# One table of places set anew for a fused attention, Fourier-mix and feed-forward kernel

## The chip, the core and the metric

The kernel runs on one core of one Trainium2 chip. The core has five engines with in-order queues: PE (TensorE, matrix products), DVE (VectorE), ACT (ScalarE), POOL (GpSimd) and SP (SyncE, which here only issues transfers). They meet at semaphores; transfers run on 16 DMA engines that all queues share. The metric is the device time of one execution in microseconds (us), lower is better. All times below are from the profiled execution or from the timed runs.

## What is computed

For a batch of 8 sequences of 576 tokens, 8 heads of 64:

```
q_d, k_d, v_d = mean over groups of 4 tokens      # 144 tokens
out_up    = repeat(softmax_attention(q_d, k_d, v_d), 4)
out_local = softmax_attention(q, k, v) where |i - j| < 4
x   = heads side by side of (out_up + out_local)  # 8 x 576 x 512
u   = x + real(fft over channels(fft over tokens(x)))
un  = (u - mean) / sqrt(var + 1e-6)
out = u + relu(un @ w1) @ w2                      # 512 -> 2048 -> 512
```

## The kernel before, in words

The work is cut into steps, each a method that issues a few instructions on one engine. Every step is put on a list by `at`, and the list is sorted and issued; so every engine gets its instructions in the order of that list, and works through them in that order. A step stands at the number that the table `TURNS` gives it (a *place*); a step that has none stands at a planned time `t`, and all steps with a place come before all without.

- **Unit** (40 of them, 5 for each batch): the local attention of 128 tokens. `load` brings q and k (`qkT`, 6 buffers), `load_v` brings v (`vaug`, 6 buffers), `sum_in` adds up groups of 4 tokens into `sums` on DVE (L603), `scores` puts a mask and the products into two banks of PSUM (L613, L620), `maxima` (DVE, L632), `exps` (ACT, L639), `transpose_p` (PE, L652), `copy_p` (ACT), `values` (PE, L680), `result` (DVE, L697 to L700; into the tiles `xa` and `xb`).
- **Pooled** (8, one for each batch): the attention over the pooled tokens, in three groups g. `scores` (L473) needs the sums of all five units of its batch; `pool_v` (L447) needs the `vaug` of all five. The group 2's `result` leaves the tile `rest` (L540), and `pack` (L564 and L553) then issues eight small transfers of it on SP. `store` issues the other pooled rows.
- **Mix** (8): the two Fourier transforms as matrix products (L793, L808, L832) with folding before and unfolding after on DVE and POOL.
- **Quarter** (64): one quarter of a feed-forward weight tile is fetched and cut into a high and a low float32r part.
- **Block** (9): the feed-forward part of 512 tokens. For each of 16 slices f of the hidden width, `first` (L1172), `high`, `low`, `second` (L1192 to L1194). Blocks 3 to 8 make the first product by seven smaller products (`open`, `more`, `close`, L1110) whose results `save` (ACT, L1130) and `combine` (DVE, L1135) join; their weights are prepared once by **Differences** (8 groups, L952 to L975), written to DRAM, and streamed back for each block.

SP issues all of the loads named and most stores, in the order of the list. An issue whose input or buffer is not ready holds back every issue behind it.

Before, the table goes up to place 1573, the first five slices of blocks 0 and 1 and eleven more of block 0 with their loads, and a few more; block 1's rest, block 2, Differences and everything after it stand at planned times.

```
place = next(places.get(name, iter(())), None)
events.append((place is None, t if place is None else place, len(events), partial(fn, *args)))
...
for *_, fn in sorted(events, key=lambda e: e[:3]):
    fn()
```

Of the kernel before, what the change touches and what calls it, by code (L numbers as in the profile page):

```python
# [26 lines left out]
    "Pooled.pool_v": (49, 130, 261, 398, 518, 677, 799, 920),  # L27
    "Pooled.copy_v": (50, 132, 263, 399, 520, 680, 800, 925),
    "Pooled.scores": (
        33, 17, 16, 163, 77, 105, 276, 200, 221, 419, 328, 348, 548, 483, 498, 675, 614, 633, 818, 744, 758,  # L30
        950, 862, 882,
    ),
    "Pooled.maxima": (
        43, 19, 20, 166, 83, 109, 283, 207, 224, 427, 332, 353, 552, 488, 511, 697, 617, 641, 823, 746, 770,
        952, 865, 891,
    ),
    "Pooled.exps": (
        46, 23, 30, 173, 86, 115, 288, 216, 231, 435, 339, 361, 558, 502, 519, 703, 620, 650, 837, 756, 780,
        954, 869, 896,
    ),  # L40
# [8 lines left out]
    "Pooled.values": (
        88, 51, 62, 198, 133, 142, 320, 264, 277, 445, 400, 413, 602, 522, 537, 727, 684, 698, 852, 803, 821,  # L50
        965, 927, 949,
    ),
    "Pooled.result": (
        93, 54, 71, 202, 155, 154, 323, 273, 284, 454, 408, 416, 605, 542, 544, 730, 694, 701, 856, 809, 826,
        972, 935, 951,
    ),
    "Pooled.store": (97, 212, 392, 463, 626, 750, 878, 975),
    "Pooled.pack": (100, 213, 342, 493, 624, 747, 871, 977),
    "Mix.half_sum": (
        120, 91, 125, 247, 252, 253, 352, 355, 372, 513, 515, 526, 636, 658, 662, 763, 762, 786, 887, 905, 904,  # L60
        1000, 1004, 1003,
    ),
    "Mix.half_difference": (
        112, 95, 111, 219, 255, 280, 356, 379, 380, 504, 529, 531, 646, 663, 665, 767, 795, 794, 885, 918, 915,
        999, 994, 1009,
    ),
    "Mix.channels": (
# [4 lines left out]
    ),  # L72
    "Mix.fold": (
# [4 lines left out]
    ),  # L78
    "Mix.split_z": (84, 137, 191, 287, 362, 382, 535, 534, 681, 686, 777, 836, 930, 921, 983, 1014),
    "Mix.sequence_z": (165, 311, 440, 573, 705, 841, 960, 1016),  # L80
    "Mix.z_high": (175, 316, 457, 587, 715, 847, 1022, 1054),
    "Mix.z_low": (182, 326, 474, 590, 720, 859, 1031, 1064),
    "Mix.sequence": (
        181, 180, 178, 179, 330, 331, 329, 327, 480, 481, 465, 466, 608, 615, 576, 586, 740, 743, 741, 739, 860,
        861, 879, 881, 1010, 1011, 987, 1007, 1071, 1070, 1107, 1102,
    ),
    "Mix.sequence_out": (193, 189, 341, 337, 484, 470, 621, 597, 755, 754, 868, 886, 1021, 1024, 1120, 1111),
    "Mix.mix": (
        239, 266, 227, 260, 350, 368, 385, 387, 366, 418, 497, 521, 500, 536, 642, 654, 631, 685, 676, 678, 772,
        804, 768, 773, 895, 900, 928, 957, 893, 901, 1069, 1072, 1068, 1029, 1131, 1157, 1186, 1214, 1185, 1213,  # L90
    ),
    "Mix.even_out": (
        262, 235, 363, 389, 390, 501, 508, 648, 634, 679, 778, 775, 898, 933, 922, 1079, 1080, 1143, 1208, 1194,
    ),
    "Mix.unfold": (
        281, 286, 270, 271, 375, 374, 404, 403, 425, 426, 539, 543, 549, 551, 660, 659, 702, 695, 689, 690, 814,
        813, 788, 787, 911, 910, 969, 968, 934, 939, 1098, 1134, 1101, 1099, 1178, 1180, 1233, 1232, 1217, 1219,
    ),
    "Mix.store_mixed": (307, 423, 625, 708, 876, 976, 1159, 1235),
    "Mix.store_local": (143, 150, 244, 309, 394, 462, 564, 572, 707, 668, 752, 783, 877, 973, 998, 1006),  # L100
    "Mix.store_ends": (496, 835, 974, 1220),
    "Unit.load": (
        2, 3, 1, 0, 7, 40, 41, 58, 57, 38, 99, 146, 147, 145, 148, 243, 149, 246, 208, 245, 396, 424, 421, 391,
        461, 568, 567, 569, 571, 595, 623, 669, 667, 709, 670, 785, 748, 832, 784, 833,
    ),
    "Unit.sum_in": (
        9, 10, 11, 12, 13, 42, 53, 64, 66, 73, 168, 172, 183, 184, 185, 282, 297, 300, 321, 324, 432, 449, 450,
        475, 477, 579, 583, 591, 593, 607, 688, 696, 733, 734, 735, 829, 830, 853, 855, 857,
    ),
    "Unit.load_v": (  # L110
        8, 36, 37, 39, 4, 5, 102, 98, 101, 103, 211, 242, 144, 209, 241, 308, 345, 393, 395, 346, 397, 490, 492,
        491, 494, 565, 627, 628, 596, 666, 751, 671, 753, 749, 782, 834, 874, 875, 872, 873,
    ),
    "Unit.scores": (
        14, 15, 25, 61, 48, 74, 104, 117, 119, 141, 199, 220, 236, 237, 319, 291, 365, 384, 420, 447, 468, 517,
        545, 585, 601, 610, 629, 652, 699, 725, 726, 781, 802, 820, 825, 864, 899, 943, 940, 956,
    ),
# [24 lines left out]
    "constants": (79,),
    "clear_yz": (136,),
    "close_b": (988,),
    "close_a": (1013,),
    "close_e": (1132,),
    "close_d": (1256,),
    "Block.load": (
        570, 798, 912, 566, 765, 884, 563, 796, 917, 344, 612, 916, 1042, 1077, 1087, 1034, 1060, 1085, 1043,
        1095, 1135, 1040, 1117, 1148, 1553, 1561, 1566, 1555, 1562, 1570, 1556, 1563, 1572, 1557, 1565, 1573,  # L150
    ),
    "Block.stats": (970, 909, 996, 971, 1137, 1162, 1164, 1179, 1571),
    "Block.norm": (991, 1005, 1028, 1048, 1150, 1175, 1177, 1216),
    "Block.turn": (1008, 1015, 1030, 1073, 1155, 1183, 1215, 1237),
    "Block.turn_high": (1020, 1038, 1057, 1081, 1171, 1191, 1225, 1240),
    "Block.turn_low": (1032, 1052, 1066, 1097, 1181, 1200, 1231, 1246),
    "Block.first": (
        1108, 1109, 1126, 1130, 1184, 1267, 1266, 1294, 1293, 1318, 1319, 1257, 1322, 1405, 1432, 1374, 1448,
        1484, 1483, 1512, 1529, 1538, 1539, 1554, 1564,
    ),  # L160
    "Block.high": (
        1112, 1115, 1153, 1168, 1209, 1273, 1269, 1303, 1307, 1351, 1361, 1381, 1391, 1415, 1440, 1417, 1460,
        1490, 1491, 1517, 1532, 1548, 1549, 1558, 1567,
    ),
    "Block.low": (
        1125, 1128, 1165, 1176, 1218, 1281, 1279, 1312, 1317, 1356, 1369, 1394, 1399, 1425, 1445, 1447, 1467,
        1497, 1499, 1526, 1534, 1550, 1551, 1559, 1568,
    ),
# [1284 lines left out]
```

## Time and profile before

| | |
|---|---|
| Timed runs | 1124.72 us median of 3 (1123.99 to 1129.9) |
| Profiled execution, span | 1124.3 us; the profile states no other time of it |
| PE busy | 1070.8 us, 95% of the span |
| DVE busy | 637.6 us, 57%; but 44 of every 50 us between 150 and 300 us |
| Attention and mix | about 0 to 320 us |
| Blocks 0 to 2 | about 300 to 590 us, blocks 3 to 8 from 590 us on |

A busy share is of the whole span or of a named window. A wait is told with the engine that waited, the operation that came next there and what released it. The granted clock of TensorE is given as a share of full speed: 1.00 is 2.4 GHz and 0.50 is 1.2 GHz.

### The profile page before, as it was taken

The numbers are of one execution on the slowest core, as the hardware profiler recorded it, in microseconds if no ns is written. First come the engines' busy times: TensorE is split into PE (matmuls) and PEld (weight loads), VectorE is DVE, ScalarE is ACT, GpSimd is POOL, SyncE is SP. The second block draws the span as 40 slices with busy tenths as digits, with TensorE's granted clock in tenths as the row PEclk, the third lists the DMA queues.
The fourth block names the chain that finished last, engine by engine and source line by source line (L and its number), as shares of the span: only waits on it lengthen the run. The fifth ranks groups of instructions, "written<-read, shape, count | busy, mean of one in ns | idle before, by whom it ended". The sixth has DMA issues, their size and how long they took to land.

```text
span 1124.3 us, 24306 instructions
## 1 busy us (share of the span) xinstructions
PE 1070.8 (95%) x9316; PEld 899.0 (80%) x9316; DVE 637.6 (57%) x1298; ACT 401.0 (36%) x1122; POOL 352.0 (31%) x501
## 2 busy tenths in 40 slices
PE   7787998999999999999999999999999999999998
PEld 5565766777778888887788889888989889889997
DVE  4778889988999885452314533443443343353333
ACT  4756565675444442132221231232232132132121
POOL 1313231233475553487331140331231331222000
PEclk9999999999999999999999999999999999999999
DMA  6545647676685444478709845955955975875641
GB/s 246 187 168 189 223 140 226 226 229 175 181 193 169 123 122 140 111 241 279 194 1 278 245 152 166 314 171 160 298 194 162 259 236 159 221 252 183 216 160 38
DMA packets 121451, 214.36 MB, mean 191 GB/s; under 512 B 14576, under 2 KB 30992, under 8 KB 121208
## 3 DMA queue, kind: packets, MB, share of 16 engines
q1 hardware_dynamic: 110056, 191.97, 52.0%
q0 software_dynamic: 11280, 20.84, 10.2%
q8 instruction: 74, 1.21, 0.4%
q14 instruction: 41, 0.34, 0.1%
HBM read 166.86 MB, written 45.42 MB: 189 GB/s over the span
## 4 chain that ended last, share of the span: by engine, by line
PE 67%; DMA 13%; DVE 9%; SPq 4%; POOL 3%; issue 3%; ACT 2%; DVEq 0%; ACTq 0%; POOLq 0%
PE banks L1110 18%; PE banks L1192 10%; PE banks L1193 10%; PE banks L1194 10%; PE banks L1172 7%; PE banks L793 3%; DMA w1l<-ut 2%; DMA qkT<-in_qk_dram 2%; DMA w1h<-ut 2%; PE banks L832 2%; PE banks L522 1%; DMA raw<-in_wq_dram 1%; DMA vaug<-in_vw_dram 1%; PE banks L1039 1%; DMA out_dram<-ut 1%
## 5 line engine op out<-in xcount | busy, mean ns | idle before, releaser
L1192 PE MATMUL banks<-w2h,hh 128*128 128x512 f32 x576 | 228.4, 397 | 0.7 <-ACT hh L1176 0.7
L1194 PE MATMUL banks<-w2h,hl 128*128 128x512 f32 x576 | 225.0, 391 | 0.8 <-DVE hl L1180 0.8
L1193 PE MATMUL banks<-w2l,hh 128*128 128x512 f32 x576 | 225.4, 391 | 0.0
L1176 ACT ACTIVATE hh<-row 128x512 fp32r<-128x512 f32 x96 | 60.6, 632 | 285.8 <-DVE row L1135 194.2
L1135 DVE TENSOR_TENSOR row<-wt,banks 128x256 f32<-128x256 f32 x192 | 80.4, 419 | 142.9 <-PE banks L1110 138.7
L1180 DVE SCALAR_TENSOR_TENSOR hl<-row,hh 128x512 fp32r<-128x512 f32 x96 | 68.9, 718 | 118.8 <-ACT hh L1176 118.8
L1194 PEld LDWEIGHTS banks<-w2h,hl 128*128 128x128 f32 x576 | 108.2, 188 | 25.5 <-DVE hl L1180 1.7
L1192 PEld LDWEIGHTS banks<-w2h,hh 128*128 128x128 f32 x576 | 108.5, 188 | 20.7 <-ACT hh L1176 1.1
L1193 PEld LDWEIGHTS banks<-w2l,hh 128*128 128x128 f32 x576 | 108.6, 188 | 19.2
L1172 PE MATMUL banks<-unT,w1h 128*128 128x512 f32 x384 | 102.3, 392 | 0.6 <-DVE unT L1048 0.6
L1172 PEld LDWEIGHTS banks<-unT,w1h 128*128 128x128 f32 x384 | 71.7, 188 | 16.4 <-DVE unT L1048 1.0
L1009 POOL DMA_DIRECT2D ut<-ux x40 | 35.7, 1034 | 152.4 <-DMA ut<-um 124.7
L1180 DVE SCALAR_TENSOR_TENSOR hl<-banks,hh 128x512 fp32r<-128x512 f32 x48 | 32.8, 688 | 77.5 <-ACT hh L1176 77.5
L639 ACT ACTIVATE sb<-banks,mx 128x64 f32<-128x64 f32 x320 | 70.0, 330 | 1.3
L1130 ACT COPY wt<-banks 128x256 f32<-128x256 f32 x96 | 35.8, 372 | 95.4 <-PE banks L1110 95.4
L793 PE MATMUL banks<-seq,f 128*128 128x290 f32 x256 | 67.0, 412 | 2.1 <-ACT sb L639 1.4
L1110 PE MATMUL banks<-w1h,w1h 128*128 128x256 f32 x384 | 62.0, 283 | 3.1 <-DMA w1h<-ut 3.0
L1110 PE MATMUL banks<-w1h,w1l 128*128 128x256 f32 x384 | 62.6, 285 | 2.4 <-DMA w1l<-ut 2.0
L1110 PE MATMUL banks<-unT,w1h 128*128 128x256 f32 x432 | 63.4, 283 | 0.0
L1110 PE MATMUL banks<-unT,w1l 128*128 128x256 f32 x432 | 63.2, 282 | 0.0
L1110 PEld LDWEIGHTS banks<-unT,w1h 128*128 128x128 f32 x432 | 59.8, 190 | 3.9
L1110 PEld LDWEIGHTS banks<-unT,w1l 128*128 128x128 f32 x432 | 59.8, 191 | 3.7
(122 smaller groups left out, 1929.1 us busy)
## 6 DMA issues: line engine op xcount, KB each, us to landing
w1l<-ut SPq DMA_DIRECT2D x96, 256.0 KB
w1h<-ut SPq DMA_DIRECT2D x96, 256.0 KB
qkT<-in_qk_dram SPq DMA_DIRECT2D x40, 512.0 KB
w1h<-ub SPq DMA_DIRECT2D x72, 256.0 KB
w1l<-ub SPq DMA_DIRECT2D x72, 256.0 KB
raw<-in_wq_dram SPq DMA_DIRECT2D x64, 256.0 KB
vaug<-in_vw_dram SPq DMA_DIRECT2D x40, 260.0 KB
out_dram<-ut SPq DMA_DIRECT2D x36, 256.0 KB
```

Of the source, the lines that this page charges most:

```text
L639: nc.scalar.activation(out=self.sb[:, hp, z], in_=self.sc[:, z, hp], func=AF.Exp, scale=0.125, bias=self.mx[:, z, hp : hp + 1],)
L793: nc.tensor.matmul(y, l, r, start=(i == 0), stop=(i == len(mms) - 1))
L1009: nc.gpsimd.dma_start(out=to, in_=ux[b][k0 : k0 + m, :], accum_op=ALU.add)
L1110: nc.tensor.matmul(into, w[:, y, c, :], both[z][:, c, :], start=(start and i == 0), stop=(i == len(mms) - 1), skip_group_check=True)
L1130: nc.scalar.copy(out=joins[k].bitcast(F32), in_=self.ps[x])
L1135: nc.vector.tensor_add(out=place(to), in0=place(a), in1=self.ps[x])
L1172: nc.tensor.matmul(hps, a[:, c, :], unT[:, x, c, :], start=(i == 0), stop=(i == len(mms) - 1))
L1176: nc.scalar.activation(out=hh, in_=self.hps[f], func=AF.Relu)
L1180: nc.vector.scalar_tensor_tensor(out=hl, in0=self.hps[f], scalar=0.0, in1=self.hh[f].bitcast(F32), op0=ALU.max, op1=ALU.subtract)
L1192: nc.tensor.matmul(acc, hh, w2h, start=start, stop=False)
L1193: nc.tensor.matmul(acc, hh, w2l, start=False, stop=False)
L1194: nc.tensor.matmul(acc, hl, w2h, start=False, stop=stop)
```

## The change

All 1574 places are replaced by 1898 new ones. New in the table are the rest of block 1, block 2, Differences, the loads and preparation of block 3, and the first six weight streams of block 3. No operation is added, taken away or altered: each engine issues the same instructions, in as great a number, in another order. Two entries, as an example:

```
     "Unit.load_v": (
-        8, 36, 37, 39, 4, 5, 102, 98, 101, 103, 211, 242, 144, 209, 241, 308, 345, 393, 395, 346, 397, 490, 492,
...
+        18, 45, 20, 49, 37, 81, 83, 105, 24, 100, 196, 162, 122, 194, 199, 363, 344, 302, 310, 312, 461, 470,
+        480, 443, 347, 555, 491, 663, 648, 625, 742, 776, 754, 746, 783, 883, 902, 855, 830, 695,
...
     "Block.second": (
-        1140, 1156, 1182, 1212, 1236, 1295, 1296, 1320, 1321, 1363, 1375, 1404, 1406, 1433, 1449, 1482, 1485,
-        1513, 1514, 1530, 1537, 1552, 1560, 1569,
...
+        1752, 1769, 1775, 1789, 1801, 1807, 1825, 1835, 1856, 1864, 1873, 1877, 1881, 1884,
```

In the changed file the table is 94 lines longer, so a line L591 of before is L685 there.

Three places show how the order moves. The first is DVE's queue from its first real work on, before the change; `sums` are the five `sum_in` of batch 0, `mx` a unit's maxima and `mxd` the pooled maxima:

```order
L603 TENSOR_REDUCE sums<-qkT 128x8x32 x2
L603 TENSOR_REDUCE sums<-qkT 128x8x15
L603 TENSOR_REDUCE sums<-qkT 128x8x17
L603 TENSOR_REDUCE sums<-qkT 128x8x32 x2
L632 TENSOR_REDUCE mx<-banks 128x8
L478 TENSOR_REDUCE mxd<-banks 128x4 x2
L632 TENSOR_REDUCE mx<-banks 128x8
```

The same place of DVE's queue after the change:

```order
L697 TENSOR_REDUCE sums<-qkT 128x8x32
L726 TENSOR_REDUCE mx<-banks 128x8
L697 TENSOR_REDUCE sums<-qkT 128x8x32 x2
L726 TENSOR_REDUCE mx<-banks 128x8
L697 TENSOR_REDUCE sums<-qkT 128x8x32
L697 TENSOR_REDUCE sums<-qkT 128x8x15
L697 TENSOR_REDUCE sums<-qkT 128x8x17
L726 TENSOR_REDUCE mx<-banks 128x8
L572 TENSOR_REDUCE mxd<-banks 128x4
```

The maxima of three units have moved in between the sums, and unit 0's block of q and k, which was issued third, is now issued first.

The second place is SP's queue around the `pack` of batch 0 (`xa<-rest` and `ud_57<-rest`, four pairs), before the change; the `vaug` behind it are those of units 8, 6 and 9:

```order
L591 DMA vaug<-in_vw_dram 128x520
L587 DMA qkT<-in_qk_dram 128x1024
L564 DMA xa<-rest 32x128
L553 DMA ud_57<-rest 29x128
...
L591 DMA vaug<-in_vw_dram 128x520 x3
L884 DMA ux_65<-xa 56x3x512
```

The same place of SP's queue after the change; the `vaug` ahead are those of units 5 and 6, the two behind those of units 9 and 7:

```order
L685 DMA vaug<-in_vw_dram 128x520 x2
L681 DMA qkT<-in_qk_dram 128x1024
L658 DMA xa<-rest 32x128
L647 DMA ud_57<-rest 29x128
...
L685 DMA vaug<-in_vw_dram 128x520 x2
L647 DMA ud_57<-odt 30x512
```

Two loads of batch 1 stand behind the `pack` in place of three, and the `rest` that the `pack` waits for is made earlier: in the new order seven steps of DVE that stood ahead of it stand behind it (the `result` of units 2 and 3, the `maxima` of unit 5 and of the pooled group 0 of batch 1, one `half_sum` and two `channels`). On PE two steps that stood ahead of `pool_v` of batch 1 stand behind it (`scores` of unit 8, `transpose_p` of unit 6).

The third place is SP's queue around the `pack` of batch 1, before the change; the `vaug` behind it are two of the five of batch 2:

```order
L564 DMA xa<-rest 32x128
L553 DMA ud_58<-rest 29x128
L331 DMA raw<-in_wq_dram 128x512
L591 DMA vaug<-in_vw_dram 128x520 x2
L587 DMA qkT<-in_qk_dram 128x1024
```

The same place of SP's queue after the change:

```order
L685 DMA vaug<-in_vw_dram 128x520
L425 DMA raw<-in_wq_dram 128x512
L685 DMA vaug<-in_vw_dram 128x520 x2
L681 DMA qkT<-in_qk_dram 128x1024 x2
L658 DMA xa<-rest 32x128
L647 DMA ud_58<-rest 29x128
```

All v of batch 2 is now asked for ahead of the `pack` of batch 1.

## Rows read from the trace of the kernel before

**Rows 1.** The page: busy time, share and instructions of each engine.

```profile
PE 1070.8 (95%) x9316; PEld 899.0 (80%) x9316; DVE 637.6 (57%) x1298; ACT 401.0 (36%) x1122; POOL 352.0 (31%) x501
```

**Rows 2.** Windows: length, PE, PEld, DVE, ACT, POOL busy (count), clock, DMA share, GB/s.

```profile
0.00:50.00 50.00, 36.54 (x773) 28.24 (x773) 28.75 (x55) 27.95 (x102) 9.31 (x24) 1.00 0.60 209
50.00:100.00 50.00, 40.63 (x699) 28.98 (x699) 39.46 (x79) 27.35 (x95) 13.73 (x18) 0.93 0.57 191
100.00:150.00 50.00, 45.02 (x768) 33.73 (x769) 42.47 (x93) 28.61 (x103) 11.85 (x19) 0.97 0.60 197
150.00:200.00 50.00, 45.77 (x826) 33.98 (x828) 45.08 (x90) 32.62 (x119) 15.56 (x22) 1.00 0.63 194
200.00:250.00 50.00, 47.54 (x915) 35.32 (x906) 44.07 (x92) 33.24 (x122) 13.78 (x18) 1.00 0.77 236
250.00:300.00 50.00, 47.37 (x816) 35.55 (x815) 44.41 (x101) 25.30 (x89) 18.54 (x25) 1.00 0.59 159
300.00:320.00 20.00, 19.41 (x87) 15.17 (x86) 18.40 (x35) 8.86 (x23) 15.46 (x23) 1.00 0.88 214
320.00:590.00 270.00, 267.32 (x1194) 218.58 (x1193) 154.35 (x295) 87.86 (x206) 146.55 (x213) 1.00 0.54 156
590.00:1124.00 534.00, 521.18 (x3263) 469.47 (x3261) 220.62 (x464) 129.22 (x272) 107.27 (x144) 1.00 0.66 203
```

**Rows 3.** Waits of PE, 0 to 320 us: total us, times, longest.

```profile
PE banks L447 <- DMA vaug<-in_vw_dram: 5.9, 3, 3.0
PE banks L473 <- DVE sums L603: 3.8, 2, 3.6
```

**Rows 4.** Timeline of DVE, 7 to 20 and 40 to 46 us: start, us, instruction, idle before.

```profile
8.28 1.22 DVE L603 TENSOR_REDUCE sums<-qkT 128x256 f32<-128x1024 f32 x1 [7.33 <-DMA qkT<-in_qk_dram]
9.83 4.66 DVE L603 TENSOR_REDUCE sums<-qkT 128x256 f32<-128x1024 f32 x5 [0.33 <-DMA qkT<-in_qk_dram]
...
43.53 0.29 DVE L540 TENSOR_TENSOR rest<-banks,rsd 128x128 f32<-128x128 f32 x1
```

**Rows 5.** Timeline of PE, 7 to 24, 44 to 60 and 98 to 108 us.

```profile
7.69 0.43 PE L613 MATMUL banks<-maskb,identb 64*64 64x256 bf16 x4 [2.23 <-DMA maskb<-in_c_mask_dram]
...
14.54 2.41 PE L473 MATMUL banks<-sums 64*64 64x160 f32 x32 [3.56 <-DVE sums L603]
...
45.91 0.66 PE L652 MATMUL banks<-ident,sb 128*128 128x128 f32 x4 [0.44 <-DVE xb L700]
...
48.47 0.73 PE L447 MATMUL banks<-vaug,poolm 128*32 128x260 f32 x4
52.24 3.02 PE L447 MATMUL banks<-vaug,poolm 128*32 128x260 f32 x16 [3.04 <-DMA vaug<-in_vw_dram]
...
101.41 0.69 PE L680 MATMUL banks<-vaug,pT 64*64 64x65 f32 x32 [1.68 <-DVE odt L540]
```

**Rows 6.** Windows of PE alone: length, busy us (count), clock, DMA share, GB/s.

```profile
50.00:52.50 2.50, 0.26 (x4) 0.73 0.88 296
52.50:55.00 2.50, 2.50 (x16) 0.50 0.87 270
```

**Rows 7.** Timeline of SP's issues, 24 to 90 us: start, us, line, transfer.

```profile
43.88 0.62 SPq L564 DMA_DIRECT2D xa<-rest  x1
...
48.23 1.82 SPq L591 DMA_DIRECT2D vaug<-in_vw_dram  x3
...
87.56 0.90 SPq L591 DMA_DIRECT2D vaug<-in_vw_dram  x2
```

**Rows 8.** Chain that ended last, 76 to 95 us: start, us, what.

```profile
77.88 6.06 DMA vaug<-in_vw_dram
```

**Rows 9.** Waits of PE, 86 to 96 us.

```profile
PE banks L447 <- DMA vaug<-in_vw_dram: 2.2, 1, 2.2
```

**Rows 10.** Groups of DVE by form, 0 to 50 us: busy, mean ns, idle before.

```profile
L632 DVE TENSOR_REDUCE mx<-banks 128x8 f32<-128x512 f32 x7 | 4.8, 683 | 0.7 <-PE banks L620 0.7
...
L700 DVE TENSOR_TENSOR xb<-banks,rs 128x512 f32<-128x512 f32 x2 | 1.4, 692 | 0.1
```

More of the change, by code (lines that the diff above doesn't have):

```diff
@@ L26 @@
 TURNS = {
-    "Pooled.pool_v": (49, 130, 261, 398, 518, 677, 799, 920),
-    "Pooled.copy_v": (50, 132, 263, 399, 520, 680, 800, 925),
+    "Pooled.pool_v": (
+        55, 125, 253, 392, 518, 667, 797, 918,
+    ),
+    "Pooled.copy_v": (
+        59, 129, 262, 399, 521, 670, 806, 926,
+    ),
     "Pooled.scores": (
-        33, 17, 16, 163, 77, 105, 276, 200, 221, 419, 328, 348, 548, 483, 498, 675, 614, 633, 818, 744, 758,
-        950, 862, 882,
+        41, 22, 34, 150, 78, 115, 263, 204, 230, 411, 346, 361, 523, 483, 501, 671, 627, 646, 803, 755, 764,
+        934, 866, 899,
@@ L48 @@
+        953, 886, 941,
     ),
     "Pooled.values": (
[L50 to L51 removed]
+        72, 62, 66, 211, 145, 151, 316, 275, 285, 446, 403, 432, 576, 527, 551, 720, 675, 717, 856, 809, 845,
+        967, 927, 947,
     ),
     "Pooled.result": (
[L54 to L56 removed]
@@ L57 @@
-    "Pooled.store": (97, 212, 392, 463, 626, 750, 878, 975),
-    "Pooled.pack": (100, 213, 342, 493, 624, 747, 871, 977),
+        79, 63, 71, 217, 147, 161, 322, 277, 297, 456, 405, 448, 580, 536, 556, 721, 679, 719, 869, 811, 857,
+        970, 935, 956,
+    ),
+    "Pooled.store": (
+        109, 187, 404, 453, 653, 768, 868, 973,
+    ),
+    "Pooled.pack": (
+        95, 229, 332, 489, 606, 734, 891, 976,
+    ),
     "Mix.half_sum": (
-        120, 91, 125, 247, 252, 253, 352, 355, 372, 513, 515, 526, 636, 658, 662, 763, 762, 786, 887, 905, 904,
-        1000, 1004, 1003,
+        108, 134, 127, 258, 237, 254, 360, 395, 373, 515, 506, 517, 642, 639, 643, 751, 788, 774, 907, 913,
+        932, 993, 980, 996,
@@ L81 @@
-    "Mix.z_high": (175, 316, 457, 587, 715, 847, 1022, 1054),
-    "Mix.z_low": (182, 326, 474, 590, 720, 859, 1031, 1064),
[4 rows of a table added]
+    ),
+    "Mix.split_z": (
+        133, 157, 189, 267, 380, 421, 468, 558, 637, 700, 787, 815, 922, 939, 1002, 1006,
+    ),
+    "Mix.sequence_z": (
+        185, 290, 458, 559, 714, 824, 986, 1015,
+    ),
+    "Mix.z_high": (
+        207, 304, 469, 573, 715, 835, 991, 1053,
+    ),
+    "Mix.z_low": (
+        214, 311, 486, 578, 725, 843, 1013, 1083,
+    ),
     "Mix.sequence": (
-        181, 180, 178, 179, 330, 331, 329, 327, 480, 481, 465, 466, 608, 615, 576, 586, 740, 743, 741, 739, 860,
-        861, 879, 881, 1010, 1011, 987, 1007, 1071, 1070, 1107, 1102,
-    ),
@@ L148 @@
+        609, 621, 628, 640, 741, 710, 730, 773, 761, 841, 864, 876, 889, 894, 946, 961, 984, 975, 992,
+    ),
+    "constants": (
+        135,
+    ),
+    "clear_yz": (
+        176,
+    ),
+    "close_b": (
+        1008,
+    ),
+    "close_a": (
+        1014,
+    ),
+    "close_e": (
+        1119,
+    ),
+    "close_d": (
+        1317,
+    ),
     "Block.load": (
-        570, 798, 912, 566, 765, 884, 563, 796, 917, 344, 612, 916, 1042, 1077, 1087, 1034, 1060, 1085, 1043,
-        1095, 1135, 1040, 1117, 1148, 1553, 1561, 1566, 1555, 1562, 1570, 1556, 1563, 1572, 1557, 1565, 1573,
-    ),
@@ L152 @@
[L152 to L156, printed above, removed]
[3 rows of a table added]
+    ),
+    "Block.stats": (
+        995, 877, 909, 890, 1131, 1163, 1192, 1158, 1655, 1620, 1649, 1610, 1806, 1823, 1814, 1837,
+    ),
+    "Block.norm": (
+        1016, 1025, 1065, 1050, 1149, 1169, 1205, 1168, 1666, 1628, 1659, 1617, 1808, 1827, 1820, 1839,
+    ),
@@ L171 @@
-        1513, 1514, 1530, 1537, 1552, 1560, 1569,
-    ),
-    "Block.finish": (1259, 1280, 1282, 1313, 1368, 1446, 1373, 1370, 1540, 1541, 1542, 1543),
-    "Block.store": (1544, 1545, 1546, 1547),
[3 rows of a table added]
+    ),
+    "Block.finish": (
+        1242, 1289, 1287, 1249, 1356, 1357, 1535, 1371, 1566, 1569, 1571, 1570, 1738, 1702, 1723, 1708, 1885,
+        1888, 1892, 1895,
+    ),
+    "Block.store": (
+        1612, 1599, 1575, 1574, 1750, 1714, 1724, 1757, 1889, 1891, 1894, 1896,
+    ),
+    "Block.turn_copy": (
+        1838, 1846, 1836, 1844,
+    ),
@@ new lines @@
+    "Block.add_up": (
+        1841, 1848,
+    ),
+    "Block.sum_high": (
+        1868, 1859, 1849, 1857, 1853, 1858, 1852, 1861,
+    ),
+    "Block.sum_low": (
+        1893, 1890, 1876, 1869, 1887, 1897, 1875, 1886,
+    ),
+    "Differences.rejoin": (
+        1549, 1559, 1609, 1657, 1690, 1729, 1753, 1793,
+    ),
+    "Differences.differ": (
+        1550, 1593, 1647, 1675, 1703, 1731, 1762, 1803,
+    ),
+    "Differences.high": (
+        1576, 1551, 1553, 1562, 1623, 1595, 1598, 1597, 1648, 1651, 1663, 1658, 1695, 1683, 1687, 1679, 1706,
+        1710, 1704, 1717, 1735, 1733, 1740, 1739, 1767, 1781, 1771, 1764, 1810, 1804, 1809, 1816,
+    ),
@@ L175 @@
+    "Differences.low": (
+        1585, 1554, 1565, 1579, 1630, 1641, 1613, 1608, 1650, 1653, 1665, 1660, 1700, 1694, 1696, 1685, 1707,
+        1713, 1719, 1721, 1742, 1749, 1743, 1744, 1776, 1797, 1780, 1786, 1813, 1817, 1812, 1828,
+    ),
+    "Differences.keep": (
[4 rows of a table added]
+    ),
+    "Block.stream": (
+        1770, 1783, 1787, 1860, 1819, 1821,
+    ),
     "Quarter.fetch": (
[4 rows of a table removed]
[4 rows of a table added]
     ),
     "Quarter.size": (
[4 rows of a table removed]
[4 rows of a table added]
     ),
     "Quarter.clamp": (
[4 rows of a table removed]
[4 rows of a table added]
     ),
     "Quarter.join": (
[4 rows of a table removed]
[4 rows of a table added]
     ),
     "Quarter.high": (
[4 rows of a table removed]
[4 rows of a table added]
```

109 lines of the change are left out of this document (57 added, 52 removed), and 82 rows, old and new, of the table TURNS.

## The prediction

> **What bounds the kernel now.** I began with the busy shares [rows 1]: PE is busy for 1070.8 of 1124.3 us, so at most 53.5 us are to be had without faster operations, and an order can't make an operation faster. The windows [rows 2] say where they lie. Of the 270 us from 320 to 590 us PE idles for 2.7 (267.32 busy), and after that, where the table reaches only the first weights, for 12.8. So the change is decided in the first 320 us: PE idles there for 13.5, 9.4, 5.0, 4.2, 2.5 and 2.6 us in the six windows of 50 us, and for 0.6 in the last 20, together 37.8. DVE is the second limit: from 150 to 300 us it is busy for 45.1, 44.1 and 44.4 of 50. Two engines near 90% that wait for each other are a stretch where an order matters, and where what one wait gives up another may take.
>
> Then the waits of PE [rows 3]. The two largest that have one cause: `pool_v` waits for v, 5.9 us in three places, and the pooled scores wait for the sums, 3.8, of which 3.6 at once. The first product waits 2.2 for the mask [rows 5]. The others are small and have many causes. The clock comes on top: after the 3.04 us that PE waits for v until 52.24 us [rows 5] the granted clock reads 0.73 and then 0.50, which is 1.2 GHz [rows 6], and the window from 50 to 100 us has 0.93 on the mean [rows 2]; against full speed 0.07 x 50 = 3.5 us are lost there, which no wait shows. The next window's 0.97 (1.5 us) has a wait of 1.68 us in it [rows 5]. The profiled execution has no time beside its span of 1124.3 us; the median of the runs is 0.4 above it, and I add that at the end.
>
> **The change, part by part.** Work removed or added: none, on no engine. So the sum is over waits.
>
> *Term 1, the start.* Today DVE gets unit 0's block at 8.28 us, as the third of the issues, and the next block 1.55 us later, at 9.83 [rows 4]; so the first issue lands, as an estimate, at 8.28 - 2 x 1.55 = 5.2. In the new order that is unit 0's. PE gains nothing directly, since its first product waits for the mask until 7.69 [rows 5], and that doesn't move. What moves is the work in the 3.56 us before the pooled scores at 14.54. The new order puts there the scores of a third unit (some 1.3 us, an estimate) and the transposes of a first (0.66, the row at 45.91): 1.9 us of work taken out of later. Against it the sums end later, since three maxima of 0.68 [rows 10] now stand between them. DVE adds unit 0's sums up to 6.4, waits for PE's scores to about 9.0, and then has 4.66 + 3 x 0.68 = 6.7: it ends at 15.7, where it ended at 14.5. That is 1.2 late, so 0.7 is left. Term 1: -0.7. Bounds: -3.6 if the wait goes whole, +1.2 if the work brought forward hides nothing.
>
> *Term 2, v of batch 1.* What is late today: `rest` is done at 43.53 + 0.29 = 43.8 [rows 4], and SP, whose next issue is `pack`, starts at 43.88. The eight issues take until 48.23; only then go three loads of v [rows 7], and PE gets the last at 52.24, 4.0 us behind. PE was there at 48.47 [rows 5]. In the new order seven steps of DVE no longer stand ahead of `rest`: two `result`, one of them with two half-sized writes (by the 0.69 of one write [rows 10], with 0.36 of two small steps ahead of it, 1.05 and 1.74), two maxima (0.68 and, on the wider pooled ones, some 0.8), a `half_sum` (0.7) and two `channels` (0.4 each), together 5.8 us as an estimate. `rest` would then be done near 38.0, `pack` issued by 42.4, and the loads behind it landed 4.0 later, at 46.4 or a little after. PE gets to `pool_v` sooner too, by the scores and the transposes that moved behind it (some 1.1 + 0.66 = 1.8) and by term 1: 48.5 - 1.8 - 0.7 = 46.0. With the second load one issue later I put the wait at 1.0 in place of 3.04. Of the clock's 3.5 I take 2.5 as saved: the wait of 1.68 stood by a loss of 1.5, and one of 1.0 may still cost that much less a third. Term 2: -2.0 - 2.5 = -4.5. Bounds: -3.0 - 3.5 = -6.5 if nothing is left of it. The other end is 0: a load of v took 6.06 us from issue to landing in a busier stretch [rows 8], and 2.1 us more than I assumed brings the whole wait back, and with it the clock. The Trainium skill (DMA: Bandwidth & Descriptors, section "Issuing engines are not separate DMA queues") says that transfers of all queues run on the same 16 engines and interleave; by that rule a load moved forward pays for what it moves into, and the term would lie nearer to 0.
>
> *Term 3, v of batch 2.* Two of the five loads go out at 87.56 [rows 7], behind the `pack` of batch 1, and `pool_v` waits 2.2 us for them [rows 9]. In the new order all five stand ahead of that `pack`. What is left of the 5.9 us after these two waits is 0.7, the size of such a wait when the loads go in time; I take -2.0, between 0 and -2.2.
>
> *Term 4, all other waits up to 320 us.* 37.8 less those of terms 1 to 3 (3.6 + 3.0 + 2.2) are 29.0 us, the mask's 2.2 and PE's own first start included. Each is set by which of two crowded queues is ahead, and I can't follow them by hand. I take 0. Bounds: if every 50 us from 50 to 300 idled like the best window (2.46), that would be 12.3 in place of 23.7; 5.2 of this is in terms 2 and 3, so -6.2. Upwards one new wait like the one for v, with its clock: 3.0 + 3.5 = +6.5.
>
> *Term 5, blocks 0 to 2.* Differences stood at planned times around the start of block 2 and is now spread over blocks 1 and 2; the loads of blocks 2 and 3 move among its steps. Work that follows back to back on PE covers them: it idles for 2.7 us in 270 [rows 2], and more can't be gained. One thing is new: block 3 has no places, so all of block 2, its last `second` too, is issued before block 3's `open`. Before, that `second` lay between `more` and `close` and covered the `save` and `combine` that `close` waits for; it is 12 products of 267.32 / 1194 = 0.224, 2.7 us, and more than the cover that is gone the wait can't be. I take 0, from -2.7 to +2.7.
>
> Sum: -0.7 - 4.5 - 2.0 + 0 + 0 = -7.2. From 1124.3 that is 1117.1; with the 0.4 to the median **1117.5 us**, 0.6% faster.
>
> **The rivals.**
>
> *A: the whole stretch gets denser.* PE's busy time counts the tail of each product, so a short wait can hide in it. The weight loads are the same instructions before and after; in the five windows from 50 to 300 us they are busy for 167.6 us, and the best window holds 35.55 [rows 2]. At that rate the 250 us would be 235.7: -14.3, terms 2 and 3 included. With the far ends of terms 1 and 5 (-3.6, -2.7) that gives -20.6, so 1104. For it: idle falls from 9.4 to 2.5 us between windows of much the same work. Against: DVE already has 89% in the best of them. The Trainium skill (Perfetto Trace Analysis, section "Identifying the Most-Contended Engine") says that matmul busy time is no good measure of the room left and that the busy share of weight loads is; by that rule the room is larger than the idle time of terms 1 to 4.
>
> *B: the waits only move.* DVE's 89% from 150 us on takes back what the first 100 us give: PE arrives sooner and waits for DVE. For it: DVE's work up to 320 us is unchanged, and its load is nearly even from 100 us on. Against: DVE itself idles for 21.2 of the first 50 us, and terms 2 and 3 are waits for transfers. Then 1119 to 1130, about 1124.
>
> *C, slower: a late v elsewhere.* In the new table `load_v` of unit 27 stands 4 places ahead of batch 5's `pool_v` (663, 667), unit 34's 14 ahead (783, 797) and unit 36's 16 ahead (902, 918). If SP is held up there as at 43.88, each costs like the one now: 3.0 + 3.5 = 6.5. One leaves 1124, two 1130.5, three 1137; it is slower from the second on. Against it: before, loads stood 3 and 5 places ahead of batch 3's `pool_v`, and all smaller waits for v are 0.7 us, so SP mostly runs ahead of its places.
>
> **How the numbers follow.** A measurement of this kernel can tell about 0.5%, 5.6 us, from no change. Chances: forecast (1108 to 1119) 0.46; A (below 1108) 0.12; B 0.23; C 0.19. Faster is the forecast and A, 0.58; same is B, 0.23; slower is C, 0.19. The range goes from just below A's 1104 to two late loads, 1103 to 1131; the likeliest case by itself has 1111 to 1119, its point with a few us of term 4 either way, cut at the bound to B.
>
> **What would show it.** Term 1: PE's pooled scores start near 15.7 us with three units' scores done. Term 2: no wait of 3 us on v near 46 us, and a clock of 1.00 from 50 to 60 us. Term 3: no wait for v between 80 and 95 us. Term 4: PE's idle time in the windows from 100 to 320 us within 3 us of the present 14.9. Term 5: block 3's first product follows block 2's last without a gap, with a wait before `close`. I am wrong if a window shows a clock of 0.50 at a new place, or if DVE's waits vanish and PE's grow.

## The result and the profile after

The changed kernel runs in 1107.91 us (median of 4 runs, 1107.39 to 1109.62) beside 1127.31 for the kernel before (4 runs, 1123.99 to 1131.04). The ratio is 0.9839 with a 95% interval of 0.9811 to 0.9866: 1.6% faster (the two medians by themselves give 0.983, inside that interval). The prediction started from 1124.72, the median of the first three of these runs. The profiled spans are 1124.3 and 1107.6 us, 16.7 us apart.

The page of the changed kernel, busy time and share of each engine:

```profile
PE 1064.3 (96%) x9316; PEld 892.8 (81%) x9316; DVE 635.5 (57%) x1298; ACT 401.4 (36%) x1122; POOL 349.3 (32%) x501
```

The same instructions, and PE is busy for 6.5 us less; its idle time fell from 53.5 to 43.3 us, 10.2 less. Together that is the 16.7. The windows of the changed kernel (columns as in [rows 2]) say where:

```profile
0.00:50.00 50.00, 36.98 (x859) 28.41 (x859) 35.36 (x66) 31.57 (x115) 12.28 (x27) 0.90 0.69 236
50.00:100.00 50.00, 47.58 (x899) 35.34 (x892) 43.50 (x100) 33.38 (x121) 11.88 (x21) 1.00 0.70 238
100.00:150.00 50.00, 46.98 (x790) 34.16 (x792) 47.94 (x94) 32.39 (x106) 16.05 (x21) 1.00 0.63 202
150.00:200.00 50.00, 47.33 (x950) 34.97 (x942) 44.59 (x97) 33.53 (x125) 13.58 (x22) 1.00 0.78 241
200.00:250.00 50.00, 48.32 (x829) 35.31 (x829) 44.16 (x95) 31.70 (x112) 17.30 (x23) 1.00 0.74 202
250.00:300.00 50.00, 48.60 (x572) 37.31 (x569) 42.58 (x97) 24.97 (x76) 27.42 (x37) 1.00 0.58 159
300.00:320.00 20.00, 18.22 (x79) 13.19 (x78) 17.58 (x33) 7.36 (x18) 11.46 (x18) 1.00 0.59 140
320.00:590.00 270.00, 264.35 (x1206) 218.40 (x1205) 146.39 (x273) 79.83 (x189) 134.38 (x196) 0.99 0.55 162
```

From 50 to 100 us PE idles for 2.4 us where it idled for 9.4, and DVE works for 43.5 where it worked for 39.5. From 320 to 590 us PE idles for 5.7 where it idled for 2.7: a little is given back there. The waits of PE up to 320 us have no row for v any more; the first four of the changed kernel are

```profile
PE banks L567 <- DVE sums L697: 4.1, 2, 2.5
PE banks L707 <- DMA maskb<-in_c_mask_dram: 3.1, 1, 3.1
PE banks L707 <- DVE odt L634: 2.5, 2, 1.6
PE banks L707 <- DVE xb L794: 2.4, 2, 1.8
```

and they answer to [rows 3]. A progress mark that can be compared between orders is the end of `pool_v`, once for each batch: start plus length of its last row in PE's timeline. For batch 1 that row is 52.24 + 3.02 = 55.3 us before [rows 5]. In the changed kernel, PE's timeline has:

```profile
15.55 1.23 PE L567 MATMUL banks<-sums 64*64 64x160 f32 x16 [2.45 <-DVE sums L697]
...
42.77 0.30 PE L707 MATMUL banks<-maskb,identb 64*64 64x256 bf16 x4 [1.85 <-DVE xb L794]
42.87 0.97 PE L714 MATMUL banks<-qkT 64*64 64x64 f32 x32
43.77 2.92 PE L541 MATMUL banks<-vaug,poolm 128*32 128x260 f32 x20
```

so it ends at 46.7, and PE comes to it without a wait for v. The table has this mark for every kernel of this text (us; the ratio is that to the kernel before):

| kernel | batch 0 | 1 | 2 | 3 | 7 | ratio (95%) |
|---|---|---|---|---|---|---|
| before | 29.2 | 55.3 | 95.3 | 133.7 | 272.5 | |
| changed | 27.0 | 46.7 | 80.5 | 116.0 | 251.0 | 0.9839 (0.9811 to 0.9866) |
| e1_v_first | 28.6 | 50.1 | 95.3 | 136.3 | 273.0 | 1.0028 (1.0012 to 1.0044) |
| e2_early | 27.1 | 45.5 | 79.0 | 122.0 | 259.1 | 0.9898 (0.9864 to 0.9932) |
| e3_late | 28.3 | 54.0 | 93.0 | 139.4 | 275.5 | 1.0097 (1.0062 to 1.0131) |
| e4_attn | 26.0 | 45.8 | 78.8 | 113.8 | 254.4 | 0.9849 (0.9812 to 0.9887) |
| e5_rest | 28.5 | 55.1 | 94.1 | 132.7 | 269.4 | 0.9985 (0.9965 to 1.0005) |
| e6_rest_v | 29.3 | 53.1 | 93.7 | 134.6 | 271.2 | 0.9980 (0.9952 to 1.0009) |
| e7_light_before | 29.0 | 55.3 | 92.8 | 131.8 | 264.7 | 0.9959 (0.9940 to 0.9979) |
| e8_light_after | 24.8 | 44.8 | 78.2 | 111.3 | 246.9 | 0.9829 (0.9793 to 0.9865) |
| e9_dma_new | 29.9 | 55.6 | 92.5 | 131.8 | 268.8 | 1.0002 (0.9985 to 1.0018) |
| e10_dma_old | 28.2 | 52.5 | 86.2 | 125.0 | 263.8 | 1.0163 (1.0137 to 1.0189) |
| e11_new200 | 26.0 | 45.2 | 81.3 | 120.0 | 257.8 | 0.9887 (0.9860 to 0.9915) |
| e12_dma_old2 | 26.7 | 49.6 | 83.3 | 124.1 | 260.1 | 0.9918 (0.9890 to 0.9945) |

The changed kernel is ahead by 2.2, 8.6, 14.8 and 17.7 us at batches 0 to 3 and by 21.5 at batch 7. Most of this is won in the first 95 us. Its lead at the end is 16.7: 4.8 us are given back behind batch 7.

### The profile page after: what moved, and what is told of

Same layout as the page of the kernel before. It is cut to its first block, busy times and chain, and to the rows that moved or that the text cites. A ratio compares the mean times of both kernels' runs of the same rounds, so it can differ in the third digit from the quotient of the medians.

```text
span 1107.6 us, 24297 instructions
## 1 busy us (share of the span) xinstructions
PE 1064.3 (96%) x9316; PEld 892.8 (81%) x9316; DVE 635.5 (57%) x1298; ACT 401.4 (36%) x1122; POOL 349.3 (32%) x501
## 3 DMA queue, kind: packets, MB, share of 16 engines
q0 software_dynamic: 11280, 20.84, 10.6%
## 4 chain that ended last, share of the span: by engine, by line
PE 71%; DMA 12%; DVE 9%; issue 3%; ACT 2%; SPq 1%; POOL 1%; DVEq 0%; ACTq 0%; POOLq 0%
PE banks L1204 19%; PE banks L1286 10%; PE banks L1287 10%; PE banks L1288 10%; PE banks L1266 8%; PE banks L887 3%; DMA w1l<-ut 3%; DMA qkT<-in_qk_dram 3%; DMA raw<-in_wq_dram 2%; PE banks L926 2%; PE banks L616 1%; DMA w1h<-ut 1%; PE banks L1133 1%; PE banks L774 1%; PE banks L746 1%
## 5 line engine op out<-in xcount | busy, mean ns | idle before, releaser
L1270 ACT ACTIVATE hh<-banks 128x512 fp32r<-128x512 f32 x48 | 28.5, 597 | 98.5 <-PE banks L1287 62.4
```

The lines of the kernel that those rows point to most:

```text
L1270: nc.scalar.activation(out=hh, in_=self.hps[f], func=AF.Relu)
```

## The experiments

The theories at the start: W, the gain is the waits for v with their clock, each worth its length (terms 2 and 3); and F, DVE is what the first 150 us wait for, and the new order hands it work earlier. The hybrids below set the places anew so that one part follows the new order and the rest the old one. In those built on the table of before a line L591 of before is L645; in e3_late and e12_dma_old2 it is L685. Rows of e7 have the lines of before.

**The loads for v alone.**

```
 "Unit.load_v": (
-    8, 36, 37, 39, 4, 5, 102, 98, 101, 103, 211, 242, 144, 209, 241,
+    8, 36, 37, 39, 4, 5, 101, 98, 100, 102, 211, 214, 144, 209, 213,
...
-"Pooled.pack": (100, 213,
+"Pooled.pack": (103, 215,
```

> The order of before with one thing moved: the loads and weight loads for v of batch 1 (u8, u6, u9) stand ahead of the pack of block 0, those of batch 2 (u14, u11) ahead of the pack of block 1. Theory W (the gain is the waits of the v matmuls for their tiles and the clock that fell in them, terms 2 and 3 of the prediction): about 6.5 us less, 1118 beside a before of 1124.5. Theory F (VectorE is what the first 150 us wait for; the new order hands it work earlier, and its idle time there fell by 16.1 us): the wait for v goes, but VectorE is fed no earlier, so the time is handed on to the next wait for VectorE: 0 to 4 us less, 1120.5 to 1124.5.

Measured: 1127.6 beside 1124.22 us, slower by 0.3%, which is less than the 0.5% taken as the limit of what can be told. PE does get its v: `pool_v` of batch 1 ends at 50.1 in place of 55.3. But at batch 2 nothing is left of it. In PE's timeline of e1_v_first:

```profile
48.27 1.78 PE L501 MATMUL banks<-vaug,poolm 128*32 128x260 f32 x20
54.78 1.78 PE L576 MATMUL banks<-vsum,ptd 128*64 128x65 f32 x32 [4.72 <-ACT vsum L506]
```

PE now waits 4.72 us for ACT's copy of what it has just computed. ACT's timeline:

```profile
52.26 0.21 ACT L689 ACTIVATE mx<-mx 128x8 f32<-128x8 f32 x1 [3.46 <-DVE mx L686]
52.50 1.75 ACT L693 ACTIVATE sb<-banks,mx 128x64 f32<-128x64 f32 x8
54.09 0.64 ACT L506 COPY vsum<-banks 128x520 f32<-128x520 f32 x1
```

The copy stands behind the `exps` of a unit, and these wait for its maxima on DVE. DVE's timeline:

```profile
49.87 1.75 DVE L798 TENSOR_TENSOR xs<-xa,xb 128x512 f32<-128x512 f32 x1 [3.49 <-DMA xa<-rest]
51.55 0.68 DVE L686 TENSOR_REDUCE mx<-banks 128x8 f32<-128x512 f32 x1
```

The maxima stand behind a `half_sum`, which waits 3.49 us for the transfers of `pack`. The kernel before has the same wait; DVE's row there, and ACT's for the same copy:

```profile
49.89 0.69 DVE L744 TENSOR_TENSOR xs<-xa,xb 128x512 f32<-128x512 f32 x1 [3.31 <-DMA xa<-rest]
```

```profile
54.28 0.59 ACT L452 COPY vsum<-banks 128x520 f32<-128x520 f32 x1 [1.06 <-PE banks L447]
```

So near 50 us two waits ended within 2.4 us of each other in the kernel before, DVE's for the pack and PE's for v, and both reach this copy. ACT stood only 1.06 us for PE's part of it: that is about what the wait for v was worth here, not its 3.04. And e1_v_first did not get even this, since its `half_sum` took 1.75 us in place of 0.69. POOL's `half_difference` of the same tiles runs beside it in both, and took 1.77 us before and 1.26 here; why one of the two is longer was not tested. Theory W falls here; for F's own number (0 to 4 us less) the run is too slow as well.

**The new order up to about batch 2, its complement, and the attention alone.** Each takes one order up to a place and the other behind it:

```
 "Pooled.pool_v": (
-    49, 130, 261, 398, 518, 677, 799, 920,   # before
+    55, 125, 253, 399, 518, 677, 799, 920,   # e2_early
+    49, 130, 261, 392, 518, 667, 797, 918,   # e3_late
+    55, 125, 253, 392, 518, 667, 796, 917,   # e4_attn
```

> The new order up to about the end of batch 2's share (the first 290 places), the order of before from there on. The lead of the new order at the pooled v of batch 2 is 14.8 us in the traces. Theory F: VectorE's idle time is won in these first 95 us and nothing later takes it back, so about 14 us less, 1110. Rival, the gain is spread over all eight batches (steadily denser matmuls): a third of it, 5 us less, 1119.

> The complement: the order of before up to the pooled v of batch 2, the new order behind it. Theory F: what is left to win is VectorE's idle time between 100 and 150 us, 5.5 us, less the 4 us that the new order gives back between 250 and 577 us: about 2 us less, 1122.5. Rival, a gain spread over all batches: 10 us less, 1114.

> The new order up to the end of the pooled attention of batch 7, the order of before for the feed-forward blocks behind it. Theory F with the give-back put down to the feed-forward order: the lead of about 21 us at batch 7 stays, 20 us less than before, 1104.5, and 3 to 4 us less than the changed kernel. Rival, the give-back is work that the lead had only put off (it comes due between 250 and 350 us in any order): 16 us less or worse, 1108 or above.

Measured: 1113.16, 1135.37 and 1108.18 us beside 1124.22. e2_early, 11 us less, is nearer to 14 than to 5: the early part carries most of the gain. Behind the cut it loses 4.6 us of its lead of 16.3, between batches 2 and 3. e3_late is slower by 11 us, which neither theory expected. Its PE waited here, and its DVE there:

```profile
127.41 1.35 PE L567 MATMUL banks<-sums 64*64 64x160 f32 x16 [7.17 <-DVE sums L697]
```

```profile
123.80 0.29 DVE L448 TENSOR_SCALAR wt<-wt 128x256 int32<-128x256 int32 x1 [5.64 <-POOL wt L440]
```

That is a wait of DVE for a weight quarter behind the cut. I read it as made by joining the two orders, which no run tests; if so, the total tells nothing of the late part. Behind it the run can be read: from batch 3 to batch 7 it needs 136.1 us, before 138.8, the changed kernel 135.0. The late rows are worth some 3 us there, and lose them again: from batch 7 to the end e3_late needs 856.0 us (span less mark), before 851.8. e4_attn is not to be told from the changed kernel: the feed-forward order adds nothing that these runs can show. The 3 to 4 us that it was expected to win on the changed kernel did not come; 1108.18 is the rival's number. Its lead at batch 7, 18.1 us, was already smaller: PE idles there for 5.1 us from 250 to 300 us, and in the changed kernel for 1.4. Part of this is a wait for v of batch 7, in the attention's new order:

```profile
252.43 1.96 PE L501 MATMUL banks<-vaug,poolm 128*32 128x260 f32 x16 [1.88 <-DMA vaug<-in_vw_dram]
```

**The chain of the pack, and the pack with v.** Since e1 had shown the second wait, a theory P: remove both.

```
 "Pooled.values": (
-    88, 51, 62,
+    73, 51, 62,
 "Pooled.result": (
-    93, 54, 71,
+    74, 54, 71,
-"Pooled.pack": (100, 213,
+"Pooled.pack": (97, 213,
```

> The order of before with one chain moved: the pooled values and the division of block 0's rest (PE and VectorE) stand right behind the result of unit 1, and the pack of block 0 ahead of its store on SP's queue; the loads for v keep their places behind the pack and so come earlier with it. Theory P (two waits end together near 50 us in before: the pooled v of batch 1 for its tiles at 52.2, and VectorE, with ScalarE behind it, for the pack at 49.9; the v loads alone showed no gain because the second stays): both go, the pooled v of batch 1 ends about 8 us earlier and 5 to 8 us stay at the end, 1118. Rival, the early gain is taken back at the next wait for VectorE as with the v loads alone: 0 to 2 us less, 1123.

> The same, and the loads for v of batches 1 and 2 moved ahead as in e1_v_first. Theory P: the pack was the first cause, so the v loads add little to e5_rest: another 0 to 2 us less, 1117. Theory W (each wait for v costs its own length): 6 us less than e5_rest, 1112.

Measured: 1123.29 and 1124.82 beside 1125.9 us, both intervals with no change in them. P's number falls. Its condition, that both waits go, was met by neither run. In e5_rest `rest` is done at 36.7 and `pack` issued at 36.76, 7 us sooner than in [rows 7], and DVE no longer waits for that pack. But the loads of v, though asked for at 45.79 (48.23 before), land no sooner. PE's row in e5_rest, and the window beside the landing:

```profile
52.86 2.27 PE L501 MATMUL banks<-vaug,poolm 128*32 128x260 f32 x16 [4.03 <-DMA vaug<-in_vw_dram]
```

```profile
47.00:50.00 3.00, 1.83 (x44) 1.10 (x43) 3.00 (x6) 2.97 (x13) 1.42 (x1) 1.00 0.94 282
```

The DMA engines are at 0.94 in these 3 us, where they stood at 0.25 in the kernel before: a load of q and k and the stores of `ud` and `ux` now lie beside v. In e6_rest_v three of four loads of v went out ahead of the store; the fourth was issued at 46.09 and PE waited 1.94 us for it. Of the 2.2 us that it won at batch 1, 1.6 are left at batch 2 and none at batch 3. At the next pack, that of batch 1, which the edit itself puts behind two loads of v, DVE waits longer than before (2.31); its timeline in e6_rest_v:

```profile
87.15 0.69 DVE L798 TENSOR_TENSOR xs<-xa,xb 128x512 f32<-128x512 f32 x1 [4.05 <-DMA xa<-rest]
```

**Less work for DVE.** The same edit in both orders:

```
-nc.vector.tensor_reduce(out=to, in_=x[:, :, a:e], axis=AX.X, op=ALU.add)
+nc.vector.tensor_reduce(out=to, in_=x[:, :, a:e, :2], axis=AX.X, op=ALU.add)
```

> The order of before, with VectorE's sums over two of the four tokens of a group instead of four (the pooled q and k are then sums of two tokens): about 24 us less work on VectorE up to 290 us. Theory F (VectorE's own time is what the first 300 us wait for): 12 us less or more, 1112. Rival (its idle time comes from when work and data reach it, not from how much work it has): 5 us less at most, 1119.

> The new order with the same lighter sums. Theory F: VectorE is busy 44 to 48 of 50 us there, so it gains at least as much as the order of before, 12 us or more, 1096. Rival: with TensorE idle for only 26 us of the first 320, 5 us less at most, 1103.

Measured: 1121.37 and 1105.62 beside 1125.9 us. DVE's group of sums in e7_light_before,

```profile
L603 DVE TENSOR_REDUCE sums<-qkT 128x256 f32<-128x512 f32 (+2 forms) x48 | 27.1, 590 | 14.6 <-DMA qkT<-in_qk_dram 10.3 <-PE banks L473 4.2
```

is 21.1 us shorter than before (48.2). Of this 4.6 us reach the end in the old order. In the new one the ratio, 0.9829, is not to be told from the changed kernel's 0.9839. Theory F falls as a matter of DVE's amount of work, from both sides. What fell with the new order is DVE's idle time, by 16.1 us in the first 150, at the same work.

**SP's row and the computing rows apart.** Theory D puts the gain in the places of the transfers, theory C in the order on the computing engines, and theory I in both together.

```
 "Unit.load_v": (
-    8, 36, 37, 39, 4, 5, 102, 98, 101, 103, 211, 242, 144, 209, 241,        # before
+    18, 39, 20, 41, 37, 81, 83, 104, 24, 100, 209, 162, 133, 207, 210,      # e9_dma_new
-    18, 45, 20, 49, 37, 81, 83, 105, 24, 100, 196, 162, 122, 194, 199,      # changed
+    8, 36, 37, 39, 4, 5, 102, 99, 101, 103, 206, 242, 127, 196, 241,        # e12_dma_old2
```

> The computing engines keep the order of before; only SP's row (loads, loads for v, packs and stores of batches 0 to 2, 46 steps) follows the new order as far as the data allow. Theory D (the transfers' places make the gain: v, the packs, the fetch of the weights ahead of them): most of e2_early's 11 us, 8 to 11 us less, 1115. Theory C (the computing rows make it: which division or maximum stands ahead of which on VectorE and ScalarE): 0 to 3 us less, 1123, as the loads and packs of e1, e5 and e6 moved alone.

> The complement: the computing engines follow the new order throughout, SP's row up to the pack of batch 1 (40 steps) keeps the order of before. Theory C: 10 to 14 us less than before, 1112. Theory D: 3 us less at most, 1122 or above. If the gain needs both rows, both runs show little.

> The changed kernel with all its places, and only SP's row up to the pack of batch 1 (40 steps) in the order of before. e10_dma_old, meant for this, had left the steps of block 2 that only the new table places at their planned times, and TensorE waited 13.7 us for block 2's normalised rows (un) in 450 to 590 us; up to batch 7 its pooled v was 8.7 us ahead of before (272.5 to 263.8), against 21.5 in the changed kernel. Theory I (rows and transfers only win together, each row alone half or nothing): the lead of about 9 us at batch 7 comes back and 5 to 9 us stay, 1117, so 9 us slower than the changed kernel. Theory C (the computing rows make the gain, the transfers only follow): 14 us or more less than before, 1110.

Measured: e9_dma_new 1124.15 beside 1124.1 us, nothing. e10_dma_old 1141.49 beside 1124.1; its end can't be used, as the expectation of e12 says, for this wait of PE between 450 and 590 us:

```profile
PE banks L1093 <- DVE un L1085: 13.7, 2, 11.8
```

e12_dma_old2, the same without that fault: 1117.96 beside 1127.28, ratio 0.9918, as theory I had put it (1117). So of the 1.6% the new computing rows with the old row of SP up to the pack of batch 1 give 0.8%, SP's new row of batches 0 to 2 alone 0.0%, and SP's row on top of the new computing rows the other 0.8%. Why SP's row wins nothing by itself at batch 1 is seen in e9_dma_new, DVE, then SP, then PE:

```profile
45.35 0.29 DVE L594 TENSOR_TENSOR rest<-banks,rsd 128x128 f32<-128x128 f32 x1
```

```profile
45.71 0.61 SPq L618 DMA_DIRECT2D xa<-rest  x1
...
50.09 1.65 SPq L645 DMA_DIRECT2D vaug<-in_vw_dram  x2
```

```profile
54.36 1.25 PE L501 MATMUL banks<-vaug,poolm 128*32 128x260 f32 x12 [3.33 <-DMA vaug<-in_vw_dram]
```

`rest` is still late, SP stands at the pack for it, and the two loads of v behind the pack are as late as ever. In e12_dma_old2 it is the other way about: `rest` is done at 33.4, `pack` goes at once, but three loads of v behind it are issued at 40.81, and later a load of q and k comes late. PE's timeline of e12_dma_old2:

```profile
46.62 3.01 PE L541 MATMUL banks<-vaug,poolm 128*32 128x260 f32 x16 [3.08 <-DMA vaug<-in_vw_dram]
...
90.47 0.88 PE L714 MATMUL banks<-qkT 64*64 64x64 f32 x32 [3.74 <-DMA qkT<-in_qk_dram]
```

Here the wait for v comes out at its length: batch 1 ends 2.9 us behind the changed kernel, with a wait of 3.08 (40 steps of SP differ between the two, so this is a reading and no test of the wait alone). The wait for q and k lies in the stretch to batch 3, which ends 8.1 us behind.

**The first 200 places alone.**

```
 "Pooled.pool_v": (
-    49, 130, 261, 398, 518, 677, 799, 920,
+    55, 125, 261, 398, 518, 677, 799, 920,
-"Pooled.pack": (100, 213, 342,
+"Pooled.pack": (95, 216, 342,
```

> The new order for the first 200 places alone (about 68 us of the new trace, a place behind the pooled v of batch 1), the order of before behind it. The lead at the pooled v of batch 1 is 8.6 us in the traces. If each stretch of the new order wins its own part and keeps it: 6 to 8 us less, 1118. If a gain is handed to the next wait as in e1, e5 and e6: 0 to 2 us less, 1123.

Measured: 1110.14 beside 1124.1 us, ratio 0.9887. That is more than either expectation: 1.1% of the changed kernel's 1.6%, from an order that is new only up to about 68 us. Its lead over the kernel before is 10.1 us at batch 1, 14.0 at batch 2 and 14.7 at batch 7. The old order behind the cut starts in a better state, wins 4 us more up to batch 2, and gives none of it back. PE's row:

```profile
42.65 2.59 PE L501 MATMUL banks<-vaug,poolm 128*32 128x260 f32 x20
```

## Why the prediction was right in its sign and too small in size

The predicted 1117.5 us lies 9.6 above the measured 1107.9, which is inside the range of 1103 to 1131; "faster" was the likeliest case. The case that I held likeliest, 1108 to 1119, is missed by 0.1 us: the result lies in rival A's band, which had 0.12. And the range reached that low by A's far ends of terms 1 and 5, which did not come; that the result lies inside it is in part luck. Step by step:

- **Term 1 (-0.7)** held in its mechanism. PE's pooled scores start at 15.55 (predicted 15.7), with the scores of three units and a first transpose ahead of them, after 2.45 us of wait in place of 3.56 [rows 5]. PE's first product waits for the mask 0.85 us longer than before, which the term had held fixed.
- **Terms 2 and 3 (-4.5 and -2.0)** had the mechanism right and were priced wrongly as separate sums. Both waits for v are gone, and `rest` is done at 33.7 where 38.0 was predicted; SP's first issue of `pack` in the changed kernel follows at once:

```profile
33.74 1.20 SPq L658 DMA_DIRECT2D xa<-rest  x1
```

e9 and e12 show each half of that chain: with `rest` late the loads behind the pack are late, with `rest` early and the old row of SP they land at 46.62 (46.4 was predicted). But in the old order the wait's removal was worth nothing, since another ended close by (e1); in the new order the numbers fit its length (e12). The end at 0 of term 2, a load that lands later beside other transfers, is what e5 shows: 7.1 us from issue to PE's start, where the term assumed 4.0. The Trainium skill (DMA: Bandwidth & Descriptors, section "Issuing engines are not separate DMA queues") says that all transfers interleave on the same 16 engines; the trace of e5_rest agrees, with v issued 2.4 us sooner and landed 0.6 us later at a DMA share of 0.94.
- **The clock in term 2** came out otherwise. The dip after the wait for v is gone: 1.00 from 50 to 150 us against 0.93 and 0.97 [rows 2], 5 us by the prediction's way of counting. That way prices too high: 0.7 of its 3.5 us come from 50 to 52.5, where PE is busy for 0.26 us [rows 6]. And the changed kernel reads 0.90 in its first 50 us, with 0.54 from 10 to 12.5 us and 0.61 from 42.5 to 45, again behind waits. I had named a clock of 0.50 at a new place as a sign of a wrong forecast. It came, in windows of 1 us of the changed kernel (PE alone, columns as in [rows 6]):

```profile
44.00:45.00 1.00, 1.00 (x12) 0.50 0.82 199
45.00:46.00 1.00, 1.00 (x10) 0.50 1.21 277
```

The kernel is faster all the same, so the sign was a poor one.
- **Term 4 (0) is the step that failed.** It was taken as 0 because I could not follow the other waits by hand. The whole change is -16.7 and the other terms sum to -7.2, so with these at their predicted size 9.5 us belong here. By the marks the split is another: the lead at batch 2 is 14.8 where terms 1 to 3 had 7.2, 6.7 more come up to batch 7, and 4.8 are given back behind it. PE's idle time in the windows from 100 to 320 us fell from 14.9 to 10.6, more than the 3 us allowed as a sign that the term holds. e11 says where most of the rest is: in the first 200 places. That each queue's next wait moved there together with the last is my reading of e1, e5 and e6 against e11; no run takes it apart. The bound of -6.2 was too near as well: it counted idle time alone, and PE's busy time fell by 6.5 us too.
- **Term 5 (0)** held at the seam that it named, and not in size. PE goes from block 2's last product (576.49) to block 3's first (576.71) without a gap. The wait before `close` is there and small; PE's timeline of the changed kernel:

```profile
576.71 0.88 PE L1204 MATMUL banks<-unT,w1h 128*128 128x256 f32 x6
...
581.19 0.98 PE L1204 MATMUL banks<-unT,w1h 128*128 128x256 f32 x6 [0.73 <-DVE row L1229]
```

PE idles for 3.0 us more between 320 and 590 us, its largest waits there 2.2 and 2.0 us, for `ut` and `un` of blocks; that is just beyond the term's bound of +2.7, and the marks give 4.8 back from batch 7 on. e4 shows that the old feed-forward order does not make the whole faster.
- **Rival A** was nearest in size, with a chance of 0.12. Its rate was 35.55 us of weight loads in 50; the changed kernel's five windows from 50 to 300 us hold 35.34, 34.16, 34.97, 35.31 and 37.31, 35.4 on the mean. The last of these holds other work (569 loads, 815 before); the four ahead of it have 34.9. Its -14.3 for that stretch, terms 2 and 3 included, was better than my terms 2 to 4 together, -6.5: the lead grows by 12.9 us from batch 1 to batch 7. Its far ends of terms 1 and 5 did not come. **Rival B**, that waits only move, is what e1, e5 and e6 show for single edits. For the whole change it was wrong: DVE does not take the time back from 150 us on. **Rival C** did not occur in the profiled execution of the changed kernel: no wait for v up to 320 us. It was near, though: e3_late, e4_attn, e8_light_after and e12_dma_old2 have the same order there, with unit 36's load behind the pack of batch 6, and PE waits at batch 7 for v for 2.3, 1.9, 2.4 and 2.1 us.

**What is shown and what is open.** Shown: the first 200 places hold most of the gain; computing rows and SP's row give half and nothing alone, and 1.6% together; single waits taken out of the old order give nothing measurable; DVE's amount of work is not the bound. Open: which of the 200 places are needed. No run took single steps out of the new order except for SP's row, and none took both waits near 50 us wholly out of the old one. That PE's busy time fell by 6.5 us is measured and its cause only partly seen (next but one section); how much of the 16.7 us is waits and how much the clock is not separated. No version beats the changed kernel by more than the runs can tell; e4_attn equals it.

## What to carry to other kernels

A wait in a stretch of crowded in-order queues need not be worth its length. Look on the other engines for a wait that ends within two or three microseconds of it, and follow what stands behind each to the place where they meet: here a wait of 3.04 us was worth at most about 1.1 while the other stayed. An order that moves many such waits can be worth more than the sum of what single moves show. Set the transfers' order and the computing order together, and try a new order by prefixes: where the lead is won shows in one mark per batch.

## What was not expected of the hardware

The granted clock of the profile can read 1.00 where PE is slow. In [rows 5] the 32 pooled products of the kernel before take 2.41 us. Its clock there, and a later row of it (PE alone):

```profile
15.00:17.50 2.50, 2.50 (x46) 1.00 1.03 401
...
24.96 1.54 PE L503 MATMUL banks<-ident,sd 128*128 128x128 f32 x6
```

e1_v_first, in the same order there, has

```profile
14.80 2.41 PE L527 MATMUL banks<-sums 64*64 64x160 f32 x32 [3.56 <-DVE sums L657]
...
24.76 0.87 PE L557 MATMUL banks<-ident,sd 128*128 128x128 f32 x6
...
15.00:17.50 2.50, 2.50 (x38) 0.50 1.04 409
```

that is, a clock of 0.50 from 15 to 17.5 us, where the kernel before reads 1.00 for the same 2.41. The six transposes at 24.76 (at 24.96, L503, in the kernel before) take 1.54 us there and 0.87 here, and the column reads 1.00 in both. By its durations, then, the kernel before ran at the slower clock up to about 27 us, though its column says otherwise, and the changed kernel's 0.90 in the first 50 us can't be read as a loss against its 1.00. PE's busy time from 20 to 30 us is 8.95 there against 6.51 in e1_v_first: 2.4 of the 6.5 us by which busy time fell can be this. By groups the fall lies in the small products of the attention: the transposes of `sd` fell from 19.7 to 17.9 us over the whole span, the mask's from 14.7 to 13.0, the units' scores from 28.9 to 27.6. And it cost almost nothing: e1_v_first, which reads 1.00 from 20 us on, ends `pool_v` of batch 0 only 0.6 us sooner, because PE waits there for others. The durations of one form of instruction are the better witness of the clock.
